# Causal attention with a max-out FFN: bound of the weights from column sums, and another order of groups, loads and decode

## The chip, the cores and the metric

The kernel runs on one core of a Trainium2 chip. The metric is the device time of one execution in microseconds (us). The engines are TensorE (PE in the profile, its weight loads PEld), VectorE (DVE), ScalarE (ACT), GpSimd (POOL) and SyncE (SP), which issues most DMAs. Each engine works through its own list of instructions in order and waits on semaphores for the others.

## The reference

For 8 batches of 8 heads, 576 positions and 64 columns a head, causal attention with a bias from cumulated positive gates, then a feed-forward layer that takes the larger of three products:

```python
scores = q @ k.T / sqrt(64)
cum = cumsum(maximum(s, 0))
scores = where(causal, -1e9, scores + minimum(-(cum[:, None] - cum[None, :]), 0))
x = softmax(scores) @ v                       # (8*576) x 512
h = maximum(maximum(x @ w1, x @ w2), x @ w3)  # 768 columns
out = h @ w_out                               # 512 columns
```

The four weight matrices arrive as 64-bit floats. Products need more than 16 bits of mantissa, so most operands stand as two 16-bit floats (high part and rest), and a product is three 16-bit products.

## The kernel before, in words

The heads go in pairs. A visit `v` is one head pair of one batch with some of its five blocks of query rows, and one block of one visit is a step `t`; there are 160 steps. The first two batches are visited twice (blocks 0 and 1 first, 2 to 4 later), the others once. In each step the main loop (L1458) does, in this order: the probabilities of step `t`, the row maximum of `t + 1`, some groups of the feed-forward layer, the scores of `t + 2`, the exponentials of `t + 1`, the jobs that are put down for this step, more groups, and the product with V. All engines get their instructions in the order in which this Python code runs; nothing reorders them.

A group is one accumulation on TensorE with its evictions: an up group (`pm`, 18 a set: six blocks of 128 hidden columns, three weights each) or a down group (`po`, 4 a set). A set is one batch's first 256 or last 320 rows. The very first set is done in plain 32 bits (`add_plain`, L1207: x, weights and h all f32), so that it can begin before the weights' scale is known. All other sets use pairs of 16-bit floats (`add_set`, L1123). Three accumulators (`ps_m`) are shared by groups and small products.

Order is set by a table, `PLAN`: `GROUPS` says for each step how many groups run before the scores and after the jobs; `moved` shifts a job by steps, by the name of its function and its numbers (`at`, L1307); `begun`, `split` and `fetched` give the steps in which a weight tile is begun, split into 16-bit parts and loaded; `KEEP` puts filler products (`keep_on`, L919) at a place of a step.

Each of the 24 weight tiles (`r0` to `r23`, 128 x 512 64-bit floats; 0 to 17 up, 18 to 23 down) is decoded in place. A 64-bit float is two 32-bit words, so every access to one word of each has a stride of 8 bytes. `decode1` (ScalarE, L1036) scales the high word into a half tile `t` (three buffers), `shift` (DVE, L1040), `low_bits` (DVE, L1044) and `sign` (DVE, L1051) make the 32-bit float, which ends in the low word. `gram1` (L1056) multiplies the upper 16 bits of each 128 x 128 block of it by themselves, all up blocks summed in one corner of a PSUM bank, all down blocks likewise. `wscale1` takes the row maximum, a product with an identity (`power`) spreads it, and `wscale2` makes the scale, a power of two at about the square root. `decode3` (ScalarE, L1105) and `decode4` (DVE, L1110) then split a tile into two 16-bit floats with that scale. Names in the trace: `s` scores, `av` the bank for products with V and for `gram1`, `rv` V tiles, `raw` q and k, `st` q, k and V of the first visits.

Of the kernel before, what the change touches and what calls it, by code (L numbers as in the profile page):

```python
# [21 lines left out]
"moved": ({('later_keys',): 1, ('load', 10): 2, ('load', 4): -2, ('load', 5): -3, ('load', 6): -4, ('load', 7): -5, ('load_v',  # L22
11): -1, ('load_v', 19): -1, ('load_v', 20): 1, ('load_v', 24): 1, ('load_v', 29): 1, ('load_v', 30): 1, ('load_v',
32): 1, ('load_v', 34): 2, ('load_v', 37): 1, ('load_v', 5): -1, ('load_v', 7): -1, ('nat_bias', 18, 1): -1,
('nat_bias', 23, 0): -1, ('nat_bias', 30, 0): 1, ('nat_bias', 34, 0): 2, ('nat_bias', 38, 0): 2, ('nat_hi', 22, 0):
-1, ('nat_hi', 25, 0): -1, ('nat_hi', 26, 0): -1, ('nat_hi', 26, 1): 1, ('nat_hi', 30, 0): -1, ('nat_hi', 30, 1): 1,
('nat_hi', 34, 0): -1, ('nat_hi', 38, 0): -1, ('nat_hi', 38, 1): 1, ('nat_own', 21, 0, 0): 1, ('nat_own', 21, 0, 1):
2, ('nat_own', 21, 1, 0): 2, ('nat_own', 21, 1, 1): 2, ('nat_own', 22, 0, 0): 2, ('nat_own', 22, 0, 1): 1, ('nat_own',
25, 0, 0): 1, ('nat_own', 25, 0, 1): 1, ('nat_own', 25, 1, 0): 2, ('nat_own', 25, 1, 1): 1, ('nat_own', 26, 0, 0): 2,
('nat_own', 26, 0, 1): 1, ('nat_own', 26, 1, 0): 1, ('nat_own', 26, 1, 1): 1, ('nat_own', 29, 0, 0): 1, ('nat_own',  # L30
29, 0, 1): 1, ('nat_own', 29, 1, 0): 1, ('nat_own', 29, 1, 1): 2, ('nat_own', 30, 0, 1): 2, ('nat_own', 30, 1, 1): 2,
('nat_own', 33, 0, 0): 1, ('nat_own', 33, 0, 1): 1, ('nat_own', 33, 1, 1): 2, ('nat_own', 34, 0, 0): 1, ('nat_own',
34, 0, 1): 2, ('nat_own', 34, 1, 0): 2, ('nat_own', 34, 1, 1): 2, ('nat_own', 37, 0, 1): 1, ('nat_own', 37, 1, 1): 2,
('nat_own', 38, 0, 0): 1, ('nat_own', 38, 0, 1): 1, ('nat_own', 38, 1, 0): 2, ('nat_own', 38, 1, 1): 1, ('pair_max',
20, 0): 2, ('pair_max', 21, 0): 1, ('pair_max', 22, 1): 2, ('pair_max', 23, 0): 2, ('pair_max', 23, 1): 1,
('pair_max', 24, 0): 1, ('pair_max', 24, 1): 1, ('pair_max', 25, 0): 1, ('pair_max', 26, 0): 1, ('pair_max', 26, 1):
1, ('pair_max', 27, 0): 2, ('pair_max', 28, 0): 1, ('pair_max', 28, 1): 1, ('pair_max', 29, 0): 2, ('pair_max', 30,
0): 3, ('pair_max', 30, 1): 3, ('pair_max', 31, 0): 1, ('pair_max', 31, 1): 1, ('pair_max', 32, 0): 2, ('pair_max',
33, 1): 1, ('pair_max', 34, 0): 2, ('pair_max', 34, 1): 2, ('pair_max', 35, 0): 2, ('pair_max', 36, 0): 1,
('pair_max', 36, 1): 1, ('pair_max', 37, 1): 1, ('pair_max', 38, 0): 2, ('pair_max', 38, 1): 2, ('pair_max', 39, 0):  # L40
2, ('pair_max', 39, 1): 1, ('pair_scale3', 3): 1, ('prep2', 10): 1, ('prep2', 9): -1, ('prep3', 5): -2, ('prep3', 7):
3, ('prep3', 8): -1, ('prep5', 11): 1, ('prep5', 15): -1, ('prep5', 17): -1, ('prep5', 18): -1, ('prep5', 4): -1,
('prep5', 7): -1, ('vmax', 20): 1, ('vmax', 21): 2, ('vmax', 22): 2, ('vmax', 24): 1, ('vmax', 25): 1, ('vmax', 26):
1, ('vmax', 30): 2, ('vmax', 32): 1, ('vmax', 33): 1, ('vmax', 34): 2, ('vmax', 36): 2, ('vmax', 37): 2, ('load_nat',
34): 1, ('decode4', 10): 1, ('prep3', 15): 1, ('nat_far', 29, 0, 1): -1, ('nat_far', 38, 0, 0): 1, ('nat_own', 24, 1,
1): 1, ('nat_bias', 37, 1): -1, ('nat_far', 23, 1, 1): -1, ('nat_own', 39, 0, 1): 1, ('nat_far', 24, 0, 1): -1,
('nat_far', 18, 1, 0): 1, ('load_nat', 31): 1, ('load_nat', 26): -2, ('nat_far', 38, 1, 0): 1, ('load_nat', 28): -1,
('nat_hi', 24, 0): 1, ('load_nat', 21): -1, ('prep2', 0): -2, ('decode4', 21): 2, ('prep4', 22): -1, ('decode3', 17):
-1, ('load_nat', 27): 1, ('nat_bias', 25, 1): 2, ('prep2', 11): 1, ('vmax', 39): 1, ('nat_bias', 22, 1): 3, ('load_v',
31): 1, ('load_nat', 36): -1, ('nat_bias', 35, 1): -2, ('nat_far', 35, 1, 1): 1, ('nat_bias', 38, 1): 1, ('nat_bias',  # L50
29, 1): 1, ('nat_hi', 17, 0): -1, ('prep4', 24): -1, ('prep5', 14): -1, ('nat_hi', 16, 0): -1, ('prep5', 38): 1,
('nat_far', 32, 1, 1): 1, ('nat_own', 31, 0, 1): 1, ('pair_scale1', 2): -1, ('nat_hi', 28, 0): 1, ('nat_far', 32, 1,
0): -1, ('nat_far', 35, 0, 0): -1, ('nat_far', 36, 1, 1): 1, ('bias4', 0): 1, ('nat_far', 21, 1, 1): 1, ('prep4', 35):
-2, ('load_w', 10): -1, ('nat_hi', 35, 0): 1, ('load_w', 7): 1, ('nat_hi', 27, 0): -1, ('nat_bias', 24, 0): 2,
('prep3', 6): -1, ('prep5', 24): -1, ('load_nat', 35): -2, ('load_nat', 39): 1, ('nat_own', 35, 1, 0): 1, ('nat_hi',
# [1520 lines left out]
```

## Time and profile before

| | |
|---|---|
| three runs | 838.65, 839.73 (median), 842.61 us |
| profiled execution | 840.53 us, of which the span from first to last instruction is 838.7 |
| PE, PEld, DVE, ACT, POOL busy | 96%, 75%, 76%, 63%, 35% of the span |
| chain that ended last | PE 79%, DVE 10%, DMA 5%, ACT 3% |
| mean granted clock of TensorE | 0.994 |

A busy share is an average over stages: the loads and the decode of the weights fall into the first 130 us, attention and feed-forward groups run side by side up to about 760 us, and the rest is groups alone. In a timeline a row is a run of like instructions of one line; its time reaches from the first start to the last end, and the bracket gives the idle time of the engine before it and what ended that.

### The profile page before, as it was taken

The page shows a single profiled execution, that of the slowest core. Times are in us where ns is not written, and L with a number is a line of the kernel's source. Part 1 is how long each engine was busy: PE and PEld are TensorE (multiplying, and loading weights), DVE is VectorE, ACT ScalarE, POOL GpSimd, SP SyncE. Part 2 cuts the span into 40 slices and gives each one's busy share as a digit, 9 for nine tenths or more (in the row PEclk, how much of TensorE's full clock was granted, in tenths as well). Part 3 has the DMA queues.
Part 4 walks back from the last instruction along what each step waited for, and adds up shares of the span by engine and source line. Part 5 has one row for each costly group of instructions (what it writes and reads, how often), then busy time and mean ns, then how long its engine had stood idle before and what let it go on. Part 6 is the DMA issues. An engine that isn't in the chain of part 4 may idle for free.

```text
span 838.7 us, 20489 instructions
## 1 busy us (share of the span) xinstructions
PE 807.0 (96%) x7719; PEld 626.8 (75%) x7719; DVE 636.4 (76%) x1562; ACT 531.6 (63%) x1458; POOL 297.3 (35%) x532
## 2 busy tenths in 40 slices
...
GB/s 352 381 75 93 89 156 201 189 166 161 148 171 148 153 153 148 184 134 162 170 175 125 142 152 197 117 134 139 165 164 103 138 122 107 98 73 72 14 13 32
DMA packets 232387, 119.86 MB, mean 143 GB/s; under 512 B 204512, under 2 KB 213216, under 8 KB 232288
## 3 DMA queue, kind: packets, MB, share of 16 engines
...
q10 hardware_dynamic: 576, 1.57, 0.5%
...
## 4 chain that ended last, share of the span: by engine, by line
PE 79%; DVE 10%; DMA 5%; ACT 3%; issue 1%; POOL 0%; SPq 0%; ACTq 0%; DVEq 0%; POOLq 0%
PE pm L1137 43%; PE po L1179 15%; PE av L1001 7%; PE s L655 6%; DMA r<-in_w_dram 2%; PE s L667 2%; DVE prl L848 2%; PE s L710 1%; PE pm L1217 1%; PE po L1239 1%; DMA lh<-fixed 1%; DVE w L1110 1%; DMA rv<-in_qkv_dram 1%; DMA raw<-in_start_dram 1%; ACT prh L845 1%
## 5 line engine op out<-in xcount | busy, mean ns | idle before, releaser
L1137 PE MATMUL pm<-x,w 128*128 128x320 f16 (+1 forms) x3240 | 422.3, 287 | 2.4 <-ACT x L1011 0.8
L1137 PEld LDWEIGHTS <-w 128*128 128x128 f16 x3240 | 312.3, 98 | 92.0 <-issue 5.4
L1154 DVE SCALAR_TENSOR_TENSOR m<-pm,m 128x320 f32<-128x320 f32 (+1 forms) x180 | 81.8, 456 | 93.6 <-PE pm L1137 82.7
L1143 POOL CAST hh<-m 128x320 f16<-128x320 f32 (+1 forms) x90 | 46.0, 512 | 296.9 <-DVE m L1154 245.3
L845 ACT ACTIVATE prh<-e,ri 128x384 f16<-128x384 f32 (+2 forms) x192 | 91.1, 522 | 82.0 <-DVE ri L820 81.6
L1179 PE MATMUL po<-hh,w 128*128 128x320 f16 (+1 forms) x720 | 140.4, 287 | 0.0
L1179 PEld LDWEIGHTS <-w 128*128 128x128 f16 x1080 | 103.7, 98 | 29.4 <-issue 1.2
L759 DVE CUSTOM_DVE_ANT_0 s<-s,later,qf 128x128 f32<-128x128 f32 (+1 forms) x192 | 103.7, 551 | 15.3 <-PE s L655 12.5
L790 ACT ACTIVATE e<-s,nm 128x128 f32<-128x128 f32 (+4 forms) x216 | 105.4, 496 | 5.1 <-DVE nm L759 3.8
L848 DVE SCALAR_TENSOR_TENSOR prl<-e,ri,prh 128x384 f16<-128x384 f32 (+2 forms) x192 | 102.8, 576 | 3.4 <-ACT prh L845 2.4
L1179 PE MATMUL po<-hl,w 128*128 128x320 f16 (+1 forms) x360 | 103.2, 287 | 0.0
L271 POOL COPY lh<-fixed 64x576 f16<-64x576 f16 x96 | 73.0, 775 | 80.7 <-DVE fixed L246 78.7
L1151 ACT ACTIVATE m<-pm 128x320 f32<-128x320 f32 (+1 forms) x90 | 36.4, 404 | 73.2 <-PE pm L1137 71.3
L1144 POOL TENSOR_TENSOR hl<-m,hh 128x320 f16<-128x320 f32 (+1 forms) x90 | 71.2, 791 | 7.4
L655 PE MATMUL s<-lh 128*128 128x128 f16 (+3 forms) x384 | 67.7, 300 | 3.9 <-DMA lh<-fixed 2.4
L1001 PEld LDWEIGHTS <-vh 128*64 128x64 f16 x1312 | 54.3, 111 | 11.7 <-issue 11.1
L1190 ACT ACTIVATE o<-po,os 128x320 f32<-128x320 f32 (+1 forms) x60 | 29.9, 499 | 48.9 <-PE po L1179 39.6
L655 PEld LDWEIGHTS <-lh 128*128 128x128 f16 x384 | 34.2, 98 | 19.1 <-POOL hl L1144 3.1
L790 ACT ACTIVATE s<-s,nm 128x512 f32<-128x512 f32 (+1 forms) x72 | 48.4, 673 | 0.0
L246 DVE SCALAR_TENSOR_TENSOR fixed<-fixed,qf,fixed 128x576 f16<-128x576 f32 x48 | 41.1, 892 | 4.3 <-ACT fixed L242 4.3
L790 ACT ACTIVATION_READ_ACCUMULATOR e<-s,nm 128x1 f32 x216 | 44.0, 204 | 0.0
L1012 DVE SCALAR_TENSOR_TENSOR x<-av,x 128x320 f16<-128x320 f32 (+1 forms) x60 | 27.1, 452 | 20.8 <-ACT x L1011 20.7
...
## 6 DMA issues: line engine op xcount, KB each, us to landing
...
```

Source lines behind the costliest of these rows:

```text
L271: nc.gpsimd.tensor_copy(out=R[v]["h"][own, j, x], in_=staged(v)[own, 3 - x])
L655: nc.tensor.matmul(ps[:, j, :nk], lhsT=w[:, c, qs], rhs=w[:, 1 - c, 0:nk], start=(x == "h" and not (lone and j)), stop=(x == "l"), skip_gr ...
L759: nc.vector.tensor_tensor_reduce(out=sc[:, j], in0=sc[:, j], in1=future[0][:, Q4 - nk:Q4], scale=n, scalar=3.0e38, op0=ALU.add, op1=ALU.mi ...
L790: nc.scalar.activation(out=to, in_=sc, func=AF.Exp, bias=nm[:, j:j + 1], scale=-1.0 if below(t) else 1.0, accum_out=sm[:, j:j + 1],)
L845: nc.scalar.activation(out=hi, in_=src, func=AF.Copy, scale=sc)
L848: nc.vector.scalar_tensor_tensor(out=lo, in0=src, scalar=sc, in1=hi, op0=ALU.mult, op1=ALU.subtract)
L1001: nc.tensor.matmul(o if ph else o.rearrange("p (i c) -> p i c", c=P), lhsT=lt, rhs=rt, start=(n < 2), stop=(n >= len(todo) - 2), skip_grou ...
L1137: nc.tensor.matmul(pm[:, :nq], lhsT=w[:, wt, kt, :], rhs=xt, start=(n == 0), stop=(n == 3 * NKT - 1))
L1143: nc.gpsimd.tensor_copy(out=st["hh"][:, ft, :nq], in_=m1[:, :nq])
L1144: nc.gpsimd.tensor_tensor(out=st["hl"][:, ft, :nq], in0=m1[:, :nq], in1=st["hh"][:, ft, :nq], op=ALU.subtract)
L1154: nc.vector.scalar_tensor_tensor(out=m1[:, :nq], in0=pm[:, :nq], scalar=HSC, in1=m1[:, :nq], op0=ALU.mult, op1=ALU.max)
L1179: nc.tensor.matmul(pm[:, :nq], lhsT=W[18 + ft][:, wt, dt, :], rhs=st[ht][:, ft, :nq], start=(n == 0), stop=(n == 3 * NFT - 1),)
```

## The change

*The bound.* `gram1` becomes `column_sums`: each block is multiplied by one column of ones, and each of the 72 up or 24 down products goes into a column of its own; the maximum is taken over these columns. It reads the low word after `low_bits`, which now holds the magnitude; the sign step puts the finished float into the high word. The scale is a power of two of that bound itself, no longer of its square root, which takes two multiplications away on DVE and two on GpSimd. The key `('gram1', 0, 5)` in `moved` stays, and no job has this name any more.

*The order.* About a quarter of the numbers in `GROUPS` and many in `moved` differ by one; `KEEP` loses 14 of 22 fillers.

```diff
-"KEEP": ({('b', 37): 2, ('d', 69): 2, ('b', 70): 18}),
+"KEEP": ({('b', 37): 2, ('b', 70): 6}),
...
+    one = const.tile([P, 1], BF16, name="one")
+    nc.gpsimd.memset(one, 1.0)
...
     def low_bits(i):
-        lo, ti = words(i)[0].bitcast(I32), half[i].bitcast(I32)
+        lo, ti = words(i)[0].bitcast(I32), half.pop(i).bitcast(I32)
         nc.vector.scalar_tensor_tensor(
-            out=ti, in0=lo, scalar=29, in1=ti, op0=ALU.logical_shift_right, op1=ALU.bitwise_or
+            out=lo, in0=lo, scalar=29, in1=ti, op0=ALU.logical_shift_right, op1=ALU.bitwise_or
         )
     def sign(i):
         lo, hi = (x.bitcast(I32) for x in words(i))
-        ti = half.pop(i).bitcast(I32)
         nc.vector.scalar_tensor_tensor(
-            out=lo, in0=hi, scalar=-(2 ** 31), in1=ti, op0=ALU.bitwise_and, op1=ALU.bitwise_or
+            out=hi, in0=hi, scalar=-(2 ** 31), in1=lo, op0=ALU.bitwise_and, op1=ALU.bitwise_or
         )
-        new[i] = words(i)[0].rearrange("p (a c) -> p a c", c=P)
+        new[i] = words(i)[1].rearrange("p (a c) -> p a c", c=P)
-    def gram1(kind, n, ids, of):
-        gr = bank[:, 3 * P:4 * P]
+    def column_sums(kind, n, ids, of):
...
-                    gr, lhsT=blk_c, rhs=blk_c, start=(n == 0 and a == 0 and c == 0),
-                    stop=(of == n + 1 and a == len(ids) - 1 and c == NKT - 1), skip_group_check=True,
+                    bank[:, o:o + 1], lhsT=top[:, c * P:(c + 1) * P], rhs=one, start=True, stop=True,
+                    skip_group_check=True,
...
-        nc.vector.tensor_reduce(out=am, in_=bank[:, 3 * P:4 * P], axis=AX.X, op=ALU.max)
-        WS[kind] = clamp(am, f"w{kind}")
+        nc.vector.tensor_reduce(out=am, in_=bank[:, 3 * P:3 * P + sums[kind]], axis=AX.X, op=ALU.max)
+        WS[kind] = clamp(am, f"w{kind}", 1, 40, 63)
...
-        nc.vector.tensor_scalar(out=sw, in0=sw, scalar1=2.0 ** -56, scalar2=None, op0=ALU.mult)
-        nc.gpsimd.tensor_scalar(out=rt, in0=rt, scalar1=2.0 ** 56, scalar2=None, op0=ALU.mult)
```

`decode3` and `decode4` read the high word instead of the low one. Of the order, three places:

SyncE's queue of loads, from the weight tile r17 on, before:

```order
L429 DMA r17_266<-in_w_dram 128x512
L192 DMA raw5_303<-in_start_dram 128x512
L429 DMA r11_309<-in_w_dram 128x512
L429 DMA r14_311<-in_w_dram 128x512
L214 DMA rv5_350<-in_qkv0_dram 128x256
L192 DMA raw6_352<-in_start_dram 128x512
L429 DMA r12_362<-in_w_dram 128x512
L429 DMA r15_364<-in_w_dram 128x512
L429 DMA r16_366<-in_w_dram 128x512
L214 DMA rv4_426<-in_qkv0_dram 128x256
```

And after:

```order
L434 DMA r17_268<-in_w_dram 128x512
L434 DMA r11_309<-in_w_dram 128x512
L434 DMA r13_311<-in_w_dram 128x512
L219 DMA rv4_370<-in_qkv0_dram 128x256
L219 DMA rv5_372<-in_qkv0_dram 128x256
L219 DMA rv7_374<-in_qkv0_dram 128x256
L197 DMA raw5_376<-in_start_dram 128x512
L434 DMA r14_384<-in_w_dram 128x512
L434 DMA r15_386<-in_w_dram 128x512
L434 DMA r16_388<-in_w_dram 128x512
```

The V tiles rv4, rv5 and rv7 now stand ahead of the q and k of visits 5 and 6 and of r14 to r16; r12 went ahead of r17, in front of these rows.

TensorE around the scores of steps 4 and 5 and the products with V of steps 2 and 3 (`av` from `p2` and `p3`), before, with the first burst of 20 bound products of r0 to r4:

```order
L690 MATMUL s4_330<-tri_103,identb_102 128x128
L894 MATMUL av_87<-p2_344,st1_92 128x128 x2
L879 MATMUL pp3_379<-dg3_372,e3_339 128x128 x4
L679 MATMUL s5_384<-st2_137,q2_250 128x256 x2
...
L690 MATMUL s5_384<-tri_103,identb_102 128x128
L1062 LDWEIGHTS r0_135
L1062 MATMUL av_87<-r0_135 128x128
...
L1062 MATMUL av_87<-r4_151 128x128
L894 MATMUL av_87<-p3_398,st1_92 128x128 x4
```

And after:

```order
L697 MATMUL s4_330<-tri_103,identb_102 128x128
L1069 LDWEIGHTS r0_137
L1069 MATMUL av_87<-one_121,r0_137 128x1
...
L1069 MATMUL av_87<-one_121,r4_153 128x1
L901 MATMUL av_87<-p2_344,st1_92 128x128 x2
L886 MATMUL pp3_401<-dg3_394,e3_339 128x128 x4
L686 MATMUL s5_406<-st2_139,q2_223 128x256 x2
...
L901 MATMUL av_87<-p3_420,st1_92 128x128 x4
```

The burst stands in front of the products with V of step 2 instead of those of step 3.

TensorE from the last up group of the first set to its second down group (`po0_0_1`), before:

```order
L1217 MATMUL pm0_0_5_2_1323<-x2_0_557,r17_266 128x256 x2
L1239 MATMUL po0_0_0_1329<-h0_0_0_748,r18_503 128x256
...
L1239 MATMUL po0_0_0_1329<-h0_0_1_1022,r23_438 128x256
L710 MATMUL s20_1336<-qk9_1118 128x512 x6
L710 MATMUL s20_1336<-kb0_179,qr0_182 128x512 x2
...
L714 MATMUL s20_1336<-tri_103,identb_102 128x128
L1239 MATMUL po0_0_1_1367<-h0_0_0_748,r18_503 128x256
```

And after:

```order
L1222 MATMUL pm0_0_5_2_1311<-x2_0_559,r17_268 128x256 x2
L717 MATMUL s20_1327<-qk9_1136 128x512 x6
L717 MATMUL s20_1327<-kb0_181,qr0_184 128x512 x2
...
L721 MATMUL s20_1327<-tri_103,identb_102 128x128
L1244 MATMUL po0_0_0_1355<-h0_0_0_748,r18_444 128x256
...
L1244 MATMUL po0_0_0_1355<-h0_0_1_1027,r23_442 128x256
L1244 MATMUL po0_0_1_1365<-h0_0_0_748,r18_444 128x256
```

The scores of step 20 went ahead of the first down group. Besides, the up groups 4_1, 4_2 and 5_0 of that set, before behind the scores of step 17, moved: 4_0 to 4_2 now stand between the scores of step 15 and the eight bound products of the last two down tiles, 5_0 behind the scores of step 16.

## Rows read from the trace of the kernel before

**Rows 1.** By stage: length, busy of PE, PEld, DVE, ACT, POOL; clock, DMA, GB/s
```profile
0.00:20.00 20.00, 10.18 (x45) 7.61 (x46) 12.68 (x28) 11.07 (x33) 3.92 (x25) 1.00 0.93 350
20.00:120.00 100.00, 88.58 (x613) 72.14 (x612) 87.39 (x197) 76.75 (x207) 6.25 (x7) 0.95 0.53 161
120.00:260.00 140.00, 138.79 (x1424) 106.62 (x1418) 122.52 (x248) 97.77 (x255) 72.42 (x120) 1.00 0.83 173
260.00:700.00 440.00, 434.08 (x4435) 336.05 (x4434) 363.31 (x963) 298.30 (x839) 180.51 (x324) 1.00 0.75 146
700.00:838.70 138.70, 135.36 (x1219) 104.42 (x1217) 50.53 (x130) 47.68 (x125) 34.23 (x58) 1.00 0.31 60
```

**Rows 2.** Timeline of VectorE, 36 to 120 us: start, us, what, [idle before, releaser]
```profile
36.32 0.74 DVE L540 TENSOR_REDUCE am<-rv 128x1 f32<-128x256 f32 x2 [1.96 <-DMA rv<-in_qkv_dram]
...
51.82 0.29 DVE L1069 TENSOR_REDUCE amwu<-av 128x1 f32<-128x128 f32 x1 [1.29 <-PE av L1062]
...
54.50 0.15 DVE L1085 TENSOR_SCALAR swu<-swu 128x1 f32<-128x1 f32 x1
...
57.32 0.43 DVE L1040 TENSOR_SCALAR t<-t 128x512 int32<-128x512 int32 x1 [2.27 <-ACT t L1036]
...
76.26 0.42 DVE L1229 TENSOR_TENSOR h<-pm,h 128x256 f32<-128x256 f32 x1 [0.69 <-PE pm L1217]
...
119.79 0.56 DVE L588 SCALAR_TENSOR_TENSOR qk<-raw,qk 128x384 fp32r<-128x384 f32 x1 [3.75 <-ACT qk L575]
```

**Rows 3.** Groups by form on VectorE, 20 to 120 us: busy, mean ns
```profile
L1051 DVE SCALAR_TENSOR_TENSOR r<-r,t 128x512 int32<-128x512 int32 x21 | 13.7, 688 | 0.1
...
L1044 DVE SCALAR_TENSOR_TENSOR t<-r,t 128x512 int32<-128x512 int32 x19 | 12.2, 683 | 0.0
```

**Rows 4.** Timeline of TensorE: bound products (L1062), 5-column products (L349), fillers (L921)
```profile
30.23 2.54 PE L1062 MATMUL av<-r 128*128 128x128 bf16 x20
...
50.13 1.57 PE L1062 MATMUL av<-r 128*128 128x128 bf16 x12 [1.15 <-ACT x L912]
...
72.44 2.05 PE L1062 MATMUL av<-r 128*128 128x128 bf16 x16 [0.36 <-DVE x L1012]
...
86.53 1.24 PE L1062 MATMUL av<-r 128*128 128x128 bf16 x8 [2.51 <-DVE r L1051]
...
170.92 0.22 PE L349 MATMUL kg<-pieces,pieces 64*128 64x5 f16 x3
...
352.45 1.17 PE L921 MATMUL av<-identb 128*128 128x128 bf16 x18
```

**Rows 5.** By source line, TensorE: ns min/median/max, first and last start us
```profile
L1062 PE MATMUL av<-r x96: 277/297/312, 30.2 to 87.5; 128*128 128x128 bf16 x96
...
L349 PE MATMUL kg<-pieces,pieces x9: 162/163/167, 170.9 to 227.6; 64*128 64x5 f16 x9
...
L921 PE MATMUL av<-identb x22: 218/219/220, 208.2 to 353.4; 128*128 128x128 bf16 x22
```

**Rows 6.** Timeline of ScalarE, 33 to 43 and 113 to 118 us
```profile
33.70 0.38 ACT L912 ACTIVATE x<-av 128x256 f32<-128x256 f32 x1 [2.27 <-PE av L894]
...
35.03 0.20 ACT L796 ACTIVATE se<-sm 128x2 f32<-128x2 f32 x1
...
42.50 0.41 ACT L569 ACTIVATE q<-raw 128x256 f32<-128x256 f32 x1
...
113.91 1.12 ACT L845 ACTIVATE prh<-e,ri 128x384 f16<-128x384 f32 x2 [1.03 <-DVE ri L820]
117.39 0.38 ACT L1245 ACTIVATE o<-po 128x256 f32<-128x256 f32 x1 [2.37 <-PE po L1239]
```

**Rows 7.** Timeline of TensorE around the first two down groups, and the third
```profile
111.04 0.71 PE L1239 MATMUL po<-h,r 128*128 128x256 f32 x2 [2.27 <-DVE h L1229]
...
113.06 4.29 PE L1239 MATMUL po<-h,r 128*128 128x256 f32 x12
...
120.09 2.87 PE L1239 MATMUL po<-h,r 128*128 128x256 f32 x12
```

More of the change, by code (lines that the diff above doesn't have):

```diff
@@ L21 @@
 PLAN = {
[L22 to L26, printed above, removed]
@@ L52 @@
[L52 to L55, printed above, removed]
-33, 0): 1, ('nat_bias', 23, 1): 2, ('nat_far', 31, 1, 1): -1, ('prep4', 23): 1, ('nat_far', 29, 1, 0): -1, ('nat_own',
@@ L72 @@
[L72 to L76 removed]
+"moved": ({('later_keys',): 1, ('load', 10): 2, ('load', 4): -2, ('load', 5): -2, ('load', 6): -3, ('load', 7): -5, ('load_v',
@@ new lines @@
+('nat_own', 35, 1, 0): 2, ('nat_hi', 33, 0): 1, ('nat_bias', 23, 1): 2, ('nat_far', 31, 1, 1): -1, ('prep4', 23): 1,
+('nat_far', 29, 1, 0): -1, ('prep4', 15): -1, ('load_v', 22): -1, ('load_v', 10): 1, ('nat_far', 35, 1, 0): -2,
+('sign', 2): 1, ('sign', 15): 1, ('nat_bias', 26, 1): -1, ('nat_own', 23, 1, 1): 2, ('prep4', 27): -1, ('load_w', 5):
+-1, ('nat_far', 28, 1, 0): 1, ('nat_far', 34, 0, 1): -1, ('nat_far', 17, 1, 1): -1, ('prep4', 10): 1, ('nat_bias', 17,
+1): -1, ('load_w', 8): -1, ('nat_own', 31, 1, 1): 2, ('prep2', 15): -1, ('pair_max', 25, 1): 1, ('nat_far', 32, 0, 0):
@@ L77 @@
+('pair_max', 32, 1): 1, ('prep5', 34): -1, ('load', 12): -1, ('nat_bias', 33, 1): -1, ('nat_own', 34, 0, 0): 1,
+('sign', 10): 1, ('nat_hi', 17, 0): -1, ('load', 9): -1, ('pair_scale3', 4): 1, ('nat_far', 22, 1, 0): -1, ('nat_far',
+23, 0, 0): -1, ('decode1', 21): -1, ('nat_far', 37, 0, 1): -1, ('prep2', 2): -1, ('prep2', 4): -1, ('nat_bias', 20,
+0): 1, ('low_bits', 2): 1, ('nat_hi', 21, 1): -1, ('load', 15): -1}),
 "begun": ({1: -3, 2: -2, 3: 0, 4: 0, 5: 1, 6: 1, 7: 2, 8: 2, 9: 2, 10: 3, 11: 3, 12: 4, 13: 6, 14: 5, 15: 4, 16: 6, 17: 6, 0:
@@ L515, in spread, with clamp @@
         QR.append(qr)
-    def clamp(am, name, n=1):
+    def clamp(am, name, n=1, low=80, high=127):
         amb = small.tile([P, n], BF16, tag=f"amb{n}", name=f"amb{name}")
         nc.vector.tensor_scalar(
-            out=amb, in0=am, scalar1=2.0 ** -80, scalar2=2.0 ** 127, op0=ALU.max, op1=ALU.min
+            out=amb, in0=am, scalar1=2.0 ** -low, scalar2=2.0 ** high, op0=ALU.max, op1=ALU.min
         )
@@ L1079, in wscale2 @@
         nc.vector.tensor_scalar(
-            out=rt.bitcast(I32), in0=mx.bitcast(I32), scalar1=1, scalar2=0x7F800000,
-            op0=ALU.logical_shift_right, op1=ALU.bitwise_and,
+            out=rt.bitcast(I32), in0=mx.bitcast(I32), scalar1=0x7F800000, scalar2=None, op0=ALU.bitwise_and
         )
```

113 lines of the change are left out of this document (60 added, 53 removed), and 20 rows, old and new, of the table PLAN.

## The prediction

> **What bounds the kernel now.** I read the busy time by stage first [rows 1]. From 120 us on TensorE is busy 138.8 of 140 us, then 434.1 of 440: there the end is the sum of TensorE's work, and only work taken off it, or one of some 7 us of scattered gaps, shortens the run. From 20 to 120 us it is busy 88.6 of 100 and its granted clock is 0.95. That is three stretches of about 3.4 us at the lower of its two levels (1.2 GHz), each behind a gap. In the same 100 us VectorE (DVE) is busy 87.4. So before 120 us the pace is set by DVE's in-order list and by what DVE waits for, and behind 120 us by TensorE. I therefore looked next for the waits in DVE's timeline [rows 2] and for who ends each, then for the costs of what the diff touches [rows 3 to 5], last for ScalarE and TensorE around two of the waits [rows 6, 7].
>
> Before 120 us DVE is idle 12.6 us, and four waits make up 7.7 of it [rows 2]: 1.96 us at 36.3 for a V tile's DMA, 1.29 us at 51.8 for the products that bound the weights, 0.69 us at 76.3 for an up group of the first set, 3.75 us at 119.8 for ScalarE. A fifth, 2.27 us at 57.3, is ScalarE's queue behind the first scaled weights, and nothing in the diff shortens it. Whatever shortens DVE's list or one of the four moves all that follows, up to the point at which TensorE is saturated, and from there the shift stays.
>
> **The change, term by term.**
>
> *Weights' bound.* There are 96 products, before and after. Before, 128x128 blocks multiply themselves: the burst of 20 at 30.23 takes 2.54 us, and less the 0.30 us of its last one that is 2.24 over 19 steps, 118 ns each [rows 4, 5]. After, the right-hand side is a column of ones and only the load of the strided block is left. No row shows that load with a one-column product. From below: the products of 5 columns with a fresh contiguous load (L349) run three in 0.22 us, and less the 0.163 of one that is 29 ns a step [rows 4, 5]. From above: 118. The fillers (L921, contiguous, 128 columns) step at (1.17-0.22)/17 = 56 ns [rows 4, 5]. A load that reads every fourth element should lie between the quick load and the present step, and I take 55. That is 63 ns off each step, 6 us of TensorE time over 96 of them, but all of it lies before 88 us [rows 5], where DVE sets the pace, so only the bursts that DVE waits for count:
> - the last burst for the up weights (12, at 50.13) ends the wait at 51.8: 11 x 63 = 0.7, with the earlier end of its last product 0.8 us; bounds 0 and 1.1;
> - the burst of 16 at 72.44 stands ahead of the up group that DVE waits for at 76.3: 15 x 63 = 0.95, of which the wait can give 0.69. I take 0.7; bounds 0 and 0.7.
>
> The other bursts are hidden under DVE's list. If DVE were not behind them, they would be worth 4 us more.
>
> *Scale.* Two multiplications on DVE go (L1085, 0.15 us, on the path of the first, since ScalarE waits for that scale), two on GpSimd that nobody waits for, and two reductions read 72 and 24 columns for 128. Together 0.3 us; bounds 0.2 and 0.5. One more memset on GpSimd in the first microseconds is hidden by the first loads.
>
> *Decode.* Both steps stay, 24 of each. The low bits now write a strided word, as the sign step did: 688 ns for 683 [rows 3]. The sign step now reads and writes strides with all three operands. Going from one strided operand to two costs 5 ns in these rows, so a third is put at 5 again: 24 x 10 ns, 0.2 us. Bounds: -0.5 and, if the third stride halved the speed, 21 x 0.6 = +12.6. I stay with the rows, where a stride costs nothing to speak of. Since the half tile is free after the low bits, the next decode on ScalarE can start one step earlier; ScalarE is idle 23 of those 100 us, so that is worth 0.
>
> *Loads.* On SyncE's queue the tile rv4 is moved ahead of raw5, raw6, r14, r15, r16 and rv5, 2.2 MB, which at 350 GB/s [rows 1] is some 6 us. It lands near 30 us, and the wait of 1.96 us at 36.3 is over before DVE gets there. What is late next? The reciprocal behind the two reductions needs the sums of step 5 from ScalarE, done at 35.23 [rows 6]. Those start behind the copy at 33.70, for which ScalarE waited 2.27 us: TensorE had the burst of 20 in front of that value product. In the new order that burst stands before the value product of step 2, where TensorE waits for ScalarE anyway, so the copy comes about 2.2 us earlier and the reciprocal is bound by DVE itself. One sign step (0.6 us) is put behind the reciprocal, too. Gain 1.9 us; bounds 0.5 (something else on the full DMA queue late) and 2.3. raw5, which is moved back, should land near 31 us, and ScalarE scales it at 42.5 [rows 6].
>
> *Expert groups.* The up groups 4_0 to 4_2, before behind the scores of steps 16 and 17, now stand before the products for the down weights, where TensorE waits 2.51 us for the sign steps [rows 4]. This fills that gap, but DVE is busy without a break there, so it only moves TensorE's idle time to where it waits for the next V scale. I take 0. The first down group goes behind step 20's scores, and this counts. Before, TensorE waits 2.27 us for the last piece of h, then runs the scores and the second down group (4.29 us, at the low clock), and ScalarE waits for that group until 117.39 [rows 6, 7]. Now the scores fill the gap, the first down group's ten early products too, and the second follows at once: 110.98 + 0.71 + 2.87 = 114.6 with the 2.87 us that the same group takes at full clock [rows 7]. ScalarE is then busy until 115.03, so the wait of 2.37 us disappears, and with it 2.3 of DVE's 3.75. If the low clock stays in this stretch, the group takes 4.29 and 1.4 are left. I take 2.0; bounds 0 and 2.4.
>
> *Fillers.* 14 of 22 go. In front of the 18 at 352.45 TensorE has no gap and none behind them, so each costs its 56 ns: 0.8 us; if they cover a wait that the trace hides, 0. Without them the clock should hold: it is 1.00 from 260 to 700 us, with 5.9 us of gaps in that stretch [rows 1].
>
> *The rest of the order.* Some forty groups, loads and preparations trade places with a neighbour behind 120 us. TensorE's work there is the same; its gaps (7.1 us) may shrink or grow. I take 0; bounds +3 and -3.
>
> Sum: 0.8 + 0.7 + 0.3 - 0.2 + 1.9 + 2.0 + 0.8 = 6.3 us. The profiled execution took 840.53 (span 838.7 and 1.8 around it), so 834.2; it lies 0.8 above the median of the runs, 839.73, and on that footing the forecast is 833.4 us.
>
> **Rivals.**
> 1. *The waits come back.* DVE is so full that a wait removed shows up as the next one: the load as one for ScalarE's decode, the down group as one for the transposed probabilities. For it: the loads run at the rate of the full DMA queue up to 42 us, and the value product behind the down group needs probabilities that DMA transposes. Against: what is late next was found, in both places, to be DVE's or ScalarE's own list, which is work and not a wait. The terms for loads and down group go, 6.3 - 3.9 = 2.4: 837.3.
> 2. *The load of the strided block sets the step.* For it: before, a load and a product of this form go at the same step, 118 ns, and load alone was never seen. Against: L349's step. The two burst terms go, 6.3 - 1.5 = 4.8: 834.9. The Trainium skill's page "TensorE: Matmul & The Clock Gate", section "LDWEIGHTS (loading the stationary operand)", gives columns / 1.2 ns for a load, an estimate of 107 ns for 128; by it the burst terms shrink to 0.3 us. The trace disagrees for contiguous blocks, 29 and 56 ns; for strided ones no run here shows it. The page "SBUF — State Buffer", section on the DMA port swizzle, says that reads at this spacing (two hits in a 16-byte line) run at full speed, and by that the 118 ns would not come from the moving operand, which speaks for this rival.
> 3. *Slower: the sign step with three strides.* 21 of them lie in the DVE-bound stretch, so each 0.1 us more costs 2.1. From 0.3 us more the gain is gone, from 0.5 us more (1.2 us instead of 0.69) the kernel is slower than can be mistaken. At half speed it would be 833.4 + 12.6 = 846. For it: no row has this form. Against: the step from one stride to two.
> 4. *More than forecast.* The low clock behind two of the three gaps goes (1.7 us each at most) and half of the gaps behind 120 us close: another 4 us, 829.4. For it: the gaps before 87 and 111 us are filled. Against: DVE sets the pace at the first.
>
> **How the numbers follow.** Forecast 0.52, with its own range 831 to 835.5; rival 1 0.20, rival 2 0.10, rival 3 0.05, rival 4 0.13. A difference under 0.5%, 4.2 us, can't be told from none here: faster means below 835.5, slower above 843.9. Faster: 0.47 of the forecast, all of rival 4, 0.08 of rival 2, 0.68 together. Same: the rest of the first two, rival 1, 0.27. Slower: 0.05. The range 829.4 to 838 leaves out rival 3, the ends of rival 1 and what goes beyond rival 4.
>
> **What would show it.** The 96 products at a step of 55 ns or less, or at 118 (rival 2). DVE without a wait on rv4 near 36 us, and the reduction of the up weights' bound near 48.5 us instead of 51.8; if it stands past 50.5, the load term is wrong. The sign step at 690 ns (rival 3: above 1000). The second down group's output copy near 111 to 112 us instead of 117.4. TensorE's work from 120 us on the same but for 0.8 us, and its gaps there between 4 and 10 us. The forecast is wrong if DVE reaches the first 16-bit up group less than 3 us earlier than now, or if gaps behind 120 us eat the shift.

## The result, and the profile after

The changed kernel takes 832.53 us (median of five runs, 831.47 to 834.75) against 839.73 (838.12 to 842.61): ratio 0.9913, interval 0.9897 to 0.993. The forecast was 833.4, in a range of 829.4 to 838. The total came out within 1 us. The working did not: by the two halves of the change, each run alone (below), gains larger than their terms stood against a loss of some 3 us that no term of the sum had.

By stage, with the columns of [rows 1]:

```profile
20.00:120.00 100.00, 87.10 (x642) 71.56 (x639) 91.30 (x203) 79.70 (x215) 8.01 (x7) 0.93 0.59 172
120.00:260.00 140.00, 137.70 (x1423) 104.99 (x1422) 121.17 (x252) 98.49 (x258) 73.09 (x123) 1.00 0.84 171
260.00:700.00 440.00, 436.60 (x4470) 339.15 (x4469) 364.57 (x965) 299.36 (x842) 187.46 (x332) 1.00 0.75 148
```

VectorE is busy 91.3 of the 100 us in which it sets the pace, for 87.4 before, and behind 120 us TensorE is as full as it was. So most of the gain had to come before 120 us, and it did. But TensorE's granted clock fell from 0.95 to 0.93 there. The clock records of the two profiled runs give the lower level (1.2 GHz) at 27.3, 88.8 and 112.6 us before, 10.2 us in all, and at 26.3, 36.6, 50.2 and 94.6 after, 13.7 in all.

VectorE's waits after, to be read beside [rows 2]:

```profile
33.43 0.74 DVE L547 TENSOR_REDUCE am<-rv 128x1 f32<-128x256 f32 x2
...
35.61 0.43 DVE L1047 TENSOR_SCALAR t<-t 128x512 int32<-128x512 int32 x1 [0.71 <-ACT t L1043]
...
39.28 0.69 DVE L771 TENSOR_REDUCE nm<-s 128x2 f32<-128x512 f32 x1 [0.77 <-PE s L697]
...
43.33 1.54 DVE L1047 TENSOR_SCALAR t<-t 128x512 int32<-128x512 int32 x3 [0.37 <-ACT t L1043]
...
50.57 0.23 DVE L1077 TENSOR_REDUCE amwu<-av 128x1 f32<-128x72 f32 x1 [0.24 <-PE av L1069]
...
74.27 0.42 DVE L1234 TENSOR_TENSOR h<-pm,h 128x256 f32<-128x256 f32 x1
...
113.39 0.56 DVE L595 SCALAR_TENSOR_TENSOR qk<-raw,qk 128x384 fp32r<-128x384 f32 x1 [1.29 <-ACT qk L582]
```

The same instruction stands earlier than before by 2.9 us at the V tile (36.32 to 33.43), by 0.2 at the decode of 43.50 (43.33 now), by 1.25 at the bound (51.82 to 50.57), by 2.0 at the up group (76.26 to 74.27) and by 6.4 at the q and k (119.79 to 113.39). The wait for rv4 is gone, and three others, 0.71, 0.77 and 0.37 us, have taken what it gave. The 0.77 is a wait for TensorE's scores, and TensorE shows why:

```profile
32.78 0.66 PE L1069 MATMUL av<-one,r 128*128 128x1 bf16 x16
33.45 0.71 PE L901 MATMUL av<-p,st 128*128 128x128 f32 x4
35.92 1.64 PE L886 MATMUL pp<-dg,e 128*128 128x128 f32 x8 [1.76 <-ACT dg L880]
37.48 1.23 PE L686 MATMUL s<-st,q 64*128 64x256 f32 x4
38.14 0.78 PE L692 MATMUL s<-kb,qr 64*128 64x256 f32 x2
38.85 0.39 PE L697 MATMUL s<-tri,identb 128*128 128x128 bf16 x2
39.04 1.56 PE L901 MATMUL av<-p,st 128*128 128x128 f32 x8
```

The burst of 16 is over in 0.66 us, TensorE waits 1.76 us, and from 36.6 to 40.0 its clock is at the lower level: the products with V at 39.04 take 1.56 us, where the same eight took 1.11 at full clock (at 29.81). The bursts of bound products themselves, as in [rows 4]:

```profile
23.65 0.80 PE L1069 MATMUL av<-one,r 128*128 128x1 bf16 x20
32.78 0.66 PE L1069 MATMUL av<-one,r 128*128 128x1 bf16 x16
41.59 0.65 PE L1069 MATMUL av<-one,r 128*128 128x1 bf16 x16
46.79 0.40 PE L1069 MATMUL av<-one,r 128*128 128x1 bf16 x8
49.93 0.53 PE L1069 MATMUL av<-one,r 128*128 128x1 bf16 x12 [1.75 <-ACT x L919]
```

Less the 0.17 us of the last product, the first burst is 0.63 us over 19 steps: 33 ns a step, for the 55 of the forecast and 118 before. Each load's own record still lasts 118 ns (median of the 96), so the loads overlap.

The two bit steps, as in [rows 3], the sign step first, now with three strides:

```profile
L1057 DVE SCALAR_TENSOR_TENSOR r<-r 128x512 int32<-128x512 int32 x19 | 12.5, 688 | 0.1
L1051 DVE SCALAR_TENSOR_TENSOR r<-r,t 128x512 int32<-128x512 int32 x19 | 12.3, 685 | 0.0
```

And ScalarE around the second down group's copy, which stood at 117.39 behind a wait of 2.37 us [rows 6]:

```profile
108.51 0.36 ACT L1250 ACTIVATE o<-po 128x256 f32<-128x256 f32 x1
109.95 1.12 ACT L852 ACTIVATE prh<-e,ri 128x384 f16<-128x384 f32 x2 [1.08 <-DVE ri L827]
110.98 0.39 ACT L1250 ACTIVATE o<-po 128x256 f32<-128x256 f32 x1
```

### The profile page after: what moved, and what is told of

Same layout as the page of the kernel before. It is cut to its first block, busy times and chain, and to the rows that moved or that the text cites. A ratio compares the mean times of both kernels' runs of the same rounds, so it can differ in the third digit from the quotient of the medians.

```text
span 829.7 us, 20468 instructions
## 1 busy us (share of the span) xinstructions
PE 799.0 (96%) x7705; PEld 621.1 (75%) x7705; DVE 634.9 (77%) x1560; ACT 531.1 (64%) x1458; POOL 299.2 (36%) x531
## 4 chain that ended last, share of the span: by engine, by line
PE 85%; DVE 8%; ACT 3%; DMA 2%; issue 1%; DVEq 0%; ACTq 0%
PE pm L1142 47%; PE po L1184 15%; PE av L1008 8%; PE s L662 6%; DMA r<-in_w_dram 2%; PE pm L1222 2%; PE s L674 2%; DVE prl L855 1%; PE s L717 1%; DVE w L1115 1%; PE po L1244 1%; PE s L737 1%; ACT t L1043 1%; ACT prh L852 1%; DVE am L547 1%
## 5 line engine op out<-in xcount | busy, mean ns | idle before, releaser
L852 ACT ACTIVATE prh<-s,ri 128x512 f16<-128x512 f32 x48 | 30.3, 683 | 21.0 <-DVE ri L827 20.9
```

The lines of the kernel that those rows point to most:

```text
L852: nc.scalar.activation(out=hi, in_=src, func=AF.Copy, scale=sc)
```

## The experiments

Two theories stood after the traces. A: the prediction's terms, each where it was put. B: the short bursts leave TensorE idle, its clock falls in more stretches before 60 us, and part of the gain is given back there. All ratios are to the kernel before, run on the same chip; "low" is the time at the lower clock before 120 us and "bound" the start of VectorE's reduction of the up bound (51.82 before), both in the profiled run.

| kernel | ratio (interval) | span | low | bound |
|---|---|---|---|---|
| before | 1 | 838.7 | 10.2 | 51.82 |
| changed | 0.9913 (0.9897 to 0.993) | 829.7 | 13.7 | 50.57 |
| sums_only | 0.9964 (0.995 to 0.9978) | 836.1 | 20.5 | 52.69 |
| order_only | 0.991 (0.9894 to 0.9926) | 831.5 | 3.4 | 51.37 |
| down_first | 0.9922 (0.9907 to 0.9938) | 832.0 | 23.9 | 51.48 |
| loads_back | 0.9918 (0.9903 to 0.9932) | 832.1 | 20.5 | 52.80 |
| fillers_back | 0.9911 (0.9896 to 0.9927) | 831.1 | 13.7 | 50.98 |
| hold_bursts | 0.9877 (0.9862 to 0.9893) | 828.6 | 6.8 | 49.25 |
| hold_357 | 0.989 (0.9871 to 0.9909) | 827.9 | 10.2 | 48.76 |
| hold_loads_back | 0.9928 (0.9912 to 0.9944) | 833.2 | 13.7 | 53.43 |
| hold_group | 0.9908 (0.9891 to 0.9925) | 828.6 | 3.4 | 48.81 |
| hold_all | 0.9915 (0.9899 to 0.9931) | 831.3 | 10.2 | 50.52 |
| sums_hold | 0.9962 (0.9947 to 0.9978) | 833.5 | 3.4 | 50.96 |

sums_only, order_only, down_first and loads_back ran on one chip; hold_bursts, hold_357 and fillers_back on a second; hold_loads_back, hold_group and hold_all on a third; sums_hold on a fourth. Two ratios of different chips compare only within their intervals, some 0.23% or 1.9 us to either side of their difference.

A trace is one execution, and the clock is not the same in each. fillers_back differs from the changed kernel only from 344 us on and down_first only from 102 us on, so they are two more traces of the same list up to there. They have the same three waits, and longer; fillers_back, first ScalarE, then VectorE:

```profile
34.61 0.66 ACT L1043 ACTIVATE t<-r 128x512 f32<-128x512 f32 x1 [1.92 <-DMA r<-in_w_dram]
35.30 0.43 DVE L1047 TENSOR_SCALAR t<-t 128x512 int32<-128x512 int32 x1 [1.02 <-ACT t L1043]
39.41 0.69 DVE L771 TENSOR_REDUCE nm<-s 128x2 f32<-128x512 f32 x1 [1.20 <-PE s L697]
43.73 1.54 DVE L1047 TENSOR_SCALAR t<-t 128x512 int32<-128x512 int32 x3 [0.64 <-ACT t L1043]
```

In down_first they are 1.12, 1.21 and 0.64 us. The first of the three is not TensorE's: ScalarE, which VectorE waits for there, waits in both for the DMA of a weight tile, and this decode stands at 35.25 to 35.73 us in every trace with the new loads, whatever the clock. Behind it VectorE is still 2.0 to 2.5 us earlier than before (37.71). So one list gave bounds from 50.57 to 51.48, 0.9 us apart, and the changed kernel's own trace, its fastest run, is the mildest of the three. Behind 131 us the new orders do not differ: from VectorE's q and k at 126.2 to 131.3 us to the end the traces of all of them take 701.7 to 702.1 us (702.7 in fillers_back), so what tells their spans apart lies ahead of that.

**The two halves.** sums_only is the changed code with the table of before, in which one key gets the new name; order_only is the code of before with the changed table, less its key for `gram1`, which would delay the first burst there. The edit of sums_only:

```diff
-('gram1', 0, 5): 1
+('column_sums', 0, 5): 1
```

> The kernel before with the column sums, the new decode and the new scale alone; the order, the loads and the fillers are those of before (the key that delays the first burst is renamed, so that it holds). Theory A (the prediction's terms: last up burst 0.8, burst of 16 0.7, scale 0.3, decode -0.2): 1.6 us less, 838.1, and VectorE's reduction of the up bound 0.8 to 1.3 us earlier than at 51.8. Theory B (shorter bursts leave TensorE idle, its clock falls to 1.2 GHz in more stretches, as in the changed kernel at 36.6 and 50.2 us, and gives the gain back): between 839.2 and 840.2, with more than three stretches at the lower clock.

> The changed kernel's order, loads and fillers with the bound products, decode and scale of before. Theory A (the prediction's terms: loads 1.9, down group 2.0, fillers 0.8): 4.7 us less, 835.0. Theory B (the load term is lost only because the short bursts let the clock fall at 36.6 us): the same 835.0, and the trace has no stretch at the lower clock between 32 and 45 us. Theory C (the load term is lost whatever the bursts are: ScalarE's decode and the products of step 5 are late next): 2.8 us less, 836.9.

The halves gave 0.36% and 0.90%, together 1.26%, and the whole change 0.87%: they do not add. The difference, 0.39% or 3.3 us, is only just clear of its interval (some 0.27% to either side). Put in another way, the order alone (0.991) is as fast as the whole change (0.9913): on top of it the column sums gave nothing that these runs can show. VectorE in sums_only:

```profile
36.73 0.74 DVE L547 TENSOR_REDUCE am<-rv 128x1 f32<-128x256 f32 x2 [2.08 <-DMA rv<-in_qkv_dram]
41.71 0.69 DVE L771 TENSOR_REDUCE nm<-s 128x2 f32<-128x512 f32 x1 [1.29 <-PE s L697]
52.69 0.23 DVE L1077 TENSOR_REDUCE amwu<-av 128x1 f32<-128x72 f32 x1 [0.26 <-PE av L1069]
117.45 0.56 DVE L595 SCALAR_TENSOR_TENSOR qk<-raw,qk 128x384 fp32r<-128x384 f32 x1 [2.12 <-ACT qk L582]
```

The wait for the bound is 0.26 for 1.29 us, as A had it, and yet the bound stands 0.87 us later than before: the clock is at the lower level for 20.5 of the 39 us from 20 to 59, and a wait of 1.29 us for scores has come. The gain of 2.6 us of span appears only behind it, and 1.6 of that at one place: the wait ahead of the q and k is 2.12 us for 3.75, with the down groups where they were, because no low clock falls on the second down group (2.81 us for 4.29). So both sides of B are in this one trace. The total, 0.9964, is more than A gave (838.1 is 0.9981) and more than B; neither had the size.

VectorE in order_only:

```profile
35.52 0.43 DVE L1045 TENSOR_SCALAR t<-t 128x512 int32<-128x512 int32 x1 [1.19 <-ACT t L1041]
43.05 1.56 DVE L1045 TENSOR_SCALAR t<-t 128x512 int32<-128x512 int32 x3 [0.65 <-ACT t L1041]
51.37 0.29 DVE L1074 TENSOR_REDUCE amwu<-av 128x1 f32<-128x128 f32 x1 [1.29 <-PE av L1067]
115.02 0.56 DVE L593 SCALAR_TENSOR_TENSOR qk<-raw,qk 128x384 fp32r<-128x384 f32 x1 [1.29 <-ACT qk L580]
```

833.28 us, less than all three theories gave. Only one low stretch is left, but it lies at 37.3 to 40.7, so B's "none between 32 and 45" fell: the long bursts thin the low stretches out, they do not keep this one away. The wait for the bound is the old 1.29 us.

**Two parts of the order.** First the edit of down_first, then that of loads_back:

```diff
-"GROUPS": step 18: (0, 2)
+"GROUPS": step 18: (1, 1)
```

```diff
-('load', 5): -2, ('load', 6): -3, ('load_v', 4): -1, ('load_v', 7): -2, ('load_w', 12): -1, ('load_w', 13): 1, ('load_w', 18): -1
+('load', 5): -3, ('load', 6): -4, ('load_v', 7): -1, ('load_w', 10): -1
-"fetched": 10: -2, 12: 1, 14: 2
+"fetched": 10: -1, 12: 2, 14: 1
```

> The changed kernel with one number of its groups changed: the first down group stands ahead of the scores of step 20 again, the second behind them, as before. Theory A (the down group's place is worth 2.0 to 2.5 us): 834.5 to 835.0, ScalarE's copy of the second down group waits over 2 us, and VectorE's wait ahead of the q and k at 113.4 us grows from 1.3 to over 3 us. Rival (the gap is only moved, VectorE's list is the same): 832.5, within 0.5.

> The changed kernel with SyncE's first 38 loads in the order of before (rv4 behind raw5, raw6, r14 to r16 again). The prediction's term: 1.9 us more, 834.4, VectorE waits some 2 us for rv4 near 34 us. Theory B (what the earlier rv4 gave was lost again by 43.5 us, where VectorE's list stands only 0.2 us earlier than before): 832.5 to 833.0, the wait for rv4 is there and the waits of 0.7 and 0.8 us behind it are gone.

Each costs 2.3 to 2.4 us of span in its profiled run, and by the ratios 0.8 and 0.4 us, which those runs can tell neither from nothing nor from the terms of 2.0 and 1.9. Of down_first's 2.3 us, 0.9 stand already at the bound, far ahead of its edit. The waits that they bring back, first of down_first, then of loads_back:

```profile
115.68 0.56 DVE L595 SCALAR_TENSOR_TENSOR qk<-raw,qk 128x384 fp32r<-128x384 f32 x1 [2.13 <-ACT qk L582]
```

```profile
36.43 0.74 DVE L547 TENSOR_REDUCE am<-rv 128x1 f32<-128x256 f32 x2 [3.20 <-DMA rv<-in_qkv_dram]
41.55 0.69 DVE L771 TENSOR_REDUCE nm<-s 128x2 f32<-128x512 f32 x1 [0.83 <-PE s L697]
```

The down group's place is worth 2.13 - 1.29 = 0.84 us of wait, not 2.0, and the wait of over 3 us that A gave did not come. The rest of what that wait lost, 3.75 - 2.13 = 1.62, is for the most part the low clock at 112.6 us before (4.29 us for the group, 2.87 at full clock [rows 7]), which is also gone in sums_only. In loads_back only the first of the three waits behind rv4 went (0.71), and from 37.8 us on VectorE's list stands 2.2 to 2.4 us behind that of the changed kernel: the term of 1.9 us is there in this trace, and B's reading of it falls. Against the three traces of the changed kernel the bound is 1.3 to 2.2 us later (52.80). By the timed runs the term is 0.4 us, with 1.9 to either side.

**Holding the clock.** hold_bursts puts fillers behind the first four bursts, hold_357 into three gaps of TensorE:

```diff
+        if kind == "u":
+            keep_on((30, 24, 24, 12, 0)[n], 2 * P)
```

```diff
-"KEEP": ({('b', 37): 2, ('b', 70): 6}),
+"KEEP": ({('b', 37): 2, ('b', 70): 6, ('a', 3): 16, ('a', 5): 22, ('a', 7): 18}),
```

> The changed kernel with filler products (128 contiguous columns, 56 ns each) behind its first four bursts of column sums: 30, 24, 24 and 12, so that TensorE is busy about as long there as with the products of before (2.5, 2.0, 2.0 and 1.0 us); the last burst, which VectorE waits for, stays short. Theory B (the short bursts let TensorE idle, its clock falls in more stretches before 56 us and what the bursts give is lost there): at most two stretches at the lower clock before 60 us instead of three, and 1.0 to 1.5 us less than the changed kernel, 831.0 to 831.5 for a kernel before at 839.7 (ratio 0.990). Rival (the clock before 60 us costs nothing since VectorE sets the pace; a longer TensorE list only delays): the same as the changed kernel or up to 1 us more, ratio 0.9913 to 0.9925.

> The changed kernel with fillers in three gaps of TensorE ahead of the transposed probabilities of steps 3, 5 and 7 (16, 22 and 18 of 56 ns, in gaps of 1.29, 1.76 and 1.54 us). Theory B: the stretch at the lower clock at 36.6 us goes, VectorE no longer waits 0.77 us for scores at 39.3, and the run is 0.7 to 1.2 us shorter than the changed kernel (ratio 0.9900 to 0.9905). Rival (fillers come too late or too long, the products behind them are delayed): ratio 0.9915 or more.

hold_bursts takes 830.08 us, hold_357 830.65. By the ratios the first is 0.9877 / 0.9913, 0.36% or 3.0 us faster than the changed kernel (1.1 to 4.9 by the intervals; B gave 1.0 to 1.5), and work was only added. Beside it on the same chip fillers_back takes 832.90 us, 2.8 us more, of which its 14 fillers are 0.8 by its trace. hold_357 is 0.23% or 1.9 us faster than the changed kernel by the ratios; in its trace the stretch at 36.6 us and the wait for scores are gone as B said, and one at 32.1 us has come. TensorE in hold_bursts from the second burst on:

```profile
31.78 0.67 PE L1069 MATMUL av<-one,r 128*128 128x1 bf16 x16
32.31 2.72 PE L928 MATMUL av<-identb 128*128 128x128 bf16 x24
34.82 0.94 PE L901 MATMUL av<-p,st 128*128 128x128 f32 x4
36.04 1.23 PE L886 MATMUL pp<-dg,e 128*128 128x128 f32 x8 [0.28 <-ACT dg L880]
37.20 0.70 PE L686 MATMUL s<-st,q 64*128 64x256 f32 x4
37.55 0.47 PE L692 MATMUL s<-kb,qr 64*128 64x256 f32 x2
37.95 0.28 PE L697 MATMUL s<-tri,identb 128*128 128x128 bf16 x2
38.07 1.11 PE L901 MATMUL av<-p,st 128*128 128x128 f32 x8
```

The transposed probabilities of step 5 start at 36.04, as in the changed kernel (35.92), but from there to the end of the products with V it takes 3.14 us for 4.68. The one low stretch of this trace before 60 us, 32.0 to 35.4, lies mostly on the fillers. VectorE follows:

```profile
35.73 0.43 DVE L1047 TENSOR_SCALAR t<-t 128x512 int32<-128x512 int32 x1 [1.70 <-ACT t L1043]
38.55 0.68 DVE L771 TENSOR_REDUCE nm<-s 128x2 f32<-128x512 f32 x1
49.25 0.23 DVE L1079 TENSOR_REDUCE amwu<-av 128x1 f32<-128x72 f32 x1 [0.25 <-PE av L1069]
```

The wait of 0.77 us is gone, that for ScalarE is 1.70 us for 0.71, and the bound stands at 49.25 instead of 50.57 (50.98 and 51.48 in the other two traces).

hold_loads_back joins the edits of hold_bursts and loads_back.

> The changed kernel with the fillers behind its first four bursts (as in the run before that held the clock) and SyncE's first loads in the order of before. Theory B (the earlier rv4 is worth its term once the clock holds; without the fillers the low clock takes it back): 1.5 to 2.2 us more than the kernel with the fillers alone (ratio 0.9877), so 0.9895 to 0.9903, and VectorE's reduction of the up bound near 51 us instead of 49.25. Theory C (another wait takes the place of the one for rv4 at any clock, ScalarE's decode 1.7 us at 35.7): at most 0.7 us more, ratio 0.9877 to 0.9885.

By the ratios the old loads cost 0.9928 / 0.9877, 0.5% or 4.3 us (2.4 to 6.2 by the intervals), and in the trace the bound is 4.2 us later (53.43). That is more than B's 1.5 to 2.2; what part of it is the low clock that came back with the wait (13.7 us for 6.8) was not separated. It is also a comparison of two chips. On the same chip ran hold_group (below), which has the new loads, the same fillers and one up group elsewhere, and against it the old loads cost 0.9928 / 0.9908, 0.2% or 1.7 us, which is B's size. The worth of the loads with the fillers is not settled between these two. Beside loads_back (0.9918, bound 52.80) the run says something else too: with the old loads the same fillers gained nothing.

hold_group adds the first edit below to hold_bursts, hold_all both:

```diff
-"GROUPS": step 16: (0, 0), step 17: (1, 1)
+"GROUPS": step 16: (1, 0), step 17: (0, 1)
```

```diff
+"KEEP": ('a', 4): 24
```

> The changed kernel with those fillers, and the up group 5_1 ahead of the scores of step 18, in TensorE's gap of 3.15 us at 93.1, instead of behind them. Theory B: the stretch at the lower clock at 93.4 us goes, TensorE's wait for the last piece of h (1.23 us at 106.3) shrinks or stays, and the run is the same or up to 0.7 us shorter than with the fillers alone (ratio 0.987 to 0.9877), since VectorE, which sets the pace there, waits only 0.29 us in that stretch. Rival (the clock there costs as much as before 60 us): 1 to 1.7 us shorter, 0.9857 to 0.9865.

> The kernel of the run above with 24 more fillers ahead of the transposed probabilities of step 4, in a gap of 1.66 us at 30.5. Theory B: no stretch at the lower clock is left before 120 us; VectorE's wait of 1.7 us for ScalarE at 35.7 shrinks if it came from that stretch: 0.3 to 1.2 us shorter than the run above. Rival (that wait is ScalarE's own list): the same within 0.3.

Neither beats hold_bursts, and hold_group's ratio, 0.9908, lies outside what either theory gave. hold_all misses what it was to do: low stretches are still there, at 37.5 and 98.9 us. hold_group is the one run of all these without a low stretch before 60 us, and VectorE there has one wait left behind rv4, stands at 41.71 us at the decode of 43.50 before, and has the earliest bound but one:

```profile
35.31 0.43 DVE L1047 TENSOR_SCALAR t<-t 128x512 int32<-128x512 int32 x1 [0.51 <-ACT t L1043]
48.81 0.23 DVE L1079 TENSOR_REDUCE amwu<-av 128x1 f32<-128x72 f32 x1 [0.25 <-PE av L1069]
```

In the stretch that it was made for the gap has only moved, as TensorE shows:

```profile
92.67 0.62 PE L737 MATMUL s<-qk 128*128 128x256 f32 x3 [1.35 <-ACT e L797]
...
98.06 0.23 PE L536 MATMUL gmv<-identb,ambv 128*128 128x128 bf16 x1 [2.60 <-DVE ambv L527]
```

The low stretch moved with it, to 99.7 us, so the run doesn't tell what the clock costs there. Its span is that of hold_bursts (828.6), but its median is 831.53, and by the ratios it is level with the changed kernel (0.9908 and 0.9913). Why the timed runs are longer is open, and with it how much of the 3.0 us of hold_bursts is the clock.

sums_hold joins sums_only and the fillers of hold_bursts.

> The kernel with the column sums, decode and scale alone in the order of before (ratio 0.9964), with the same fillers (30, 24, 24, 12) behind its first four bursts. Theory B (what the short bursts cost is TensorE's clock before 59 us, 20 us of it at the lower level): at most 7 us at the lower clock before 60 us, VectorE's reduction of the up bound at 50.5 to 51.0 us instead of 52.7, and 1 to 2 us less than without the fillers, ratio 0.9941 to 0.9952. Rival (the fillers helped the changed kernel by its own order of loads and preparations, not by the clock): 0.9955 to 0.9975.

This one is split. The trace does what B said: one low stretch of 3.4 us for 20.5, the bound at 50.96 for 52.69, the span 2.6 us shorter. The timed runs do not: 0.9962 against 0.9964, outside the 0.9941 to 0.9952 of B and inside the 0.9955 to 0.9975 of the rival. The profiled run (835.33 us) is one of the shorter of its twelve (834.78 to 838.46). In the old order the wait for rv4 still stands behind the first bursts (1.31 us in this trace), so what is won before 36 us has no effect; whether that is all, is open.

**Clock and time over all runs.** Each run lists its mean granted clock, and (1 - clock) x 2 x span is its time at the lower level. The five runs of the changed kernel follow it but for the middle two: 0.991 at 831.47 us, 0.986 and 0.988 at 832.21 and 832.53, 0.980 at 834.46 and 834.75. Over the 123 runs shown here and of before beside them, each against the mean of its own group, a run is 0.20 us longer for each us at the lower clock (correlation 0.60); in sums_only, down_first, loads_back, fillers_back and hold_bursts, with four to six runs each, there is hardly any such trend. The changed kernel has 25 us of it on average, hold_bursts 6, before 10. Between kernels it does not settle the time: sums_hold has 6 us of it for 20 in sums_only at the same ratio, hold_loads_back 12 for 21 in loads_back at a ratio 0.1% higher, and hold_group 8 for the 25 of the changed kernel at 0.05% less.

**Fillers and steps.** fillers_back has the fillers of before, dissect other operands in the products of before:

```diff
-"KEEP": ({('b', 37): 2, ('b', 70): 6}),
+"KEEP": ({('b', 37): 2, ('d', 69): 2, ('b', 70): 18}),
```

> The changed kernel with the 14 fillers of before put back (two at step 69, 18 instead of 6 at step 70). The prediction's term: 14 x 56 ns = 0.8 us more, TensorE's end 0.8 us later by the trace with no new gap. Rival (the fillers cover a wait): 0.

Behind the eighteen fillers TensorE's list stands 0.8 us later against the changed kernel in the trace (a shift of 0.59 ahead of them, 1.38 behind). The timed difference, 0.9911 against 0.9913, can't resolve it.

```diff
-                    gr, lhsT=blk_c, rhs=blk_c, start=(n == 0 and a == 0 and c == 0),
+                    gr, lhsT=identb if of == 5 and n == 1 else blk_c, rhs=identb if of == 5 and n in (0, 2) else blk_c,
+                    start=(of == 5 and n < 3) or (n == (3 if of == 5 else 0) and a == 0 and c == 0),
```

> The kernel before with other operands in three of its bursts for the up weights: the first (20) and third (16) load the strided block and multiply 128 contiguous columns of the identity, the second (16) loads the contiguous identity and multiplies the strided block; the bound is taken from the other bursts alone. Theory (what costs is the strided moving operand; the load is hidden behind it): 56 ns a step in the first and third, 118 in the second. Rival (a strided load costs more than a contiguous one, up to the old step): near 118 in the first and third, 56 in the second.

The first three bursts:

```profile
29.85 1.28 PE L1062 MATMUL av<-identb,r 128*128 128x128 bf16 x20
33.43 2.02 PE L1062 MATMUL av<-r,identb 128*128 128x128 bf16 x16
41.91 1.06 PE L1062 MATMUL av<-identb,r 128*128 128x128 bf16 x16
```

Less the last product (0.22 us with contiguous columns, 0.30 with strided ones [rows 5]), the strided load with contiguous columns takes 1.06 / 19 = 56 ns a step, the contiguous load with strided columns 1.72 / 15 = 115. So the old step of 118 was the strided moving operand alone.

## Why the prediction came out, point by point

- *Last up burst and burst of 16.* Right in size. The wait for the bound shrank by 1.05 us (0.8 forecast), the wait of 0.69 at 76.3 is gone (0.7). The step was mis-sized, 33 ns for 55, without effect, since both waits were over by then. Rival 2 is refuted by the step and by the kernel that took it apart. The Trainium skill's page "TensorE: Matmul & The Clock Gate", section "LDWEIGHTS (loading the stationary operand)", gives columns / 1.2 ns for a load, an estimate of 107 ns; as a bound on the step it disagrees with the 33 ns here. The Trainium skill's page "SBUF — State Buffer", section "Door 1: The DMA port swizzle", has reads with two hits in a 16-byte line at full bandwidth; the moving operand at this spacing took 115 ns for 56, which disagrees too.
- *Scale, decode.* Right: a multiplication of 0.15 us less on the path, 0.06 off the first reduction, the sign step at 688 ns as forecast. Rival 3 is refuted.
- *Loads: the step that failed, as a reading of what comes next.* The text said that behind rv4 comes DVE's own work, so that 1.9 us would stay, and that a bound later than 50.5 us would show it wrong. It stood at 50.57, and later in the two other traces of this list. The copy on ScalarE came 2.1 us earlier as forecast (31.61 for 33.70) and VectorE's reductions 2.9 us, but then ScalarE and TensorE were late, 1.85 us in three waits (2.9 and 3.0 in the other two traces). Rival 1 described this. The first wait goes back to the DMA of a weight tile and leaves 2.0 to 2.5 us of the gain; the other two take the rest, down to 0.2 us or nothing at the decode of 43.50. What rival 1 did not name is the clock behind these two: in hold_group, with no low stretch before 60 us, they are absent, that decode is 1.8 us earlier than before, and the bound stands at 48.81, near the 48.5 of the forecast. The size of 1.9 us is not refuted: taking the loads back moved the bound by 1.3 to 2.2 us in the traces, and by the ratios it cost 0.4 us without the fillers and 1.7 or 4.3 with them.
- *The missing term.* The prediction took TensorE's bursts before 88 us as hidden and looked at the clock only as something that filled gaps could give back (rival 4). The other sign was not priced: 96 products that are 85 ns shorter leave TensorE idle ahead of products that VectorE waits for. The traces show such waits, and hold_bursts and hold_group, with the fillers behind the bursts, have the bound 1.3 to 2.7 us earlier than the three traces of the changed kernel. In time hold_bursts puts it at 3.0 us and hold_357 at 1.9, but hold_group at 0.4, and hold_loads_back and sums_hold, against their kernels without fillers, at nothing. So it is shown that the low clock delays what VectorE waits for. How much of the 3.3 us that the halves lose together comes from it, is not shown.
- *Expert groups.* The forecast 2.0 for the down group came as 2.46 on the wait ahead of the q and k (3.75 to 1.29), the copy at 110.98 for a forecast of 111 to 112. But 0.84 of it is the place and 1.62 for the most part the clock; the text had counted the full clock into its 2.0, with the low clock as a case in which 1.4 would be left.
- *Fillers.* Right by the trace, 0.8 us.
- *The rest of the order.* Put at 0, bounds 3 either way: TensorE's gaps behind 120 us went from 7.1 to 5.7 us, 1.4 gained. With the 6.4 us at 113.39 and the fillers that makes 8.6 of the 9.0 us between the two profiled spans; that of the changed kernel is its fastest run, and the medians differ by 7.2.

So the sum was right by luck: by the halves the gains were 3.0 us for terms of 1.6 and 7.6 us for terms of 4.7, and a loss of 3.3 us where the two meet was left out. The shortest median of these is that of hold_bursts, the change with 90 fillers more, at 830.08 us.
